# Talking-heads attention and gMLP: scores in query chunks of 64, 128, 128, 128 instead of 120, 120, 120, 88, the 64 as four 64x64 tiles

## The chip, the cores and the metric

The kernel runs on one core of one Trainium2 chip. The metric is the device time of a whole run in microseconds (us). The engines are TensorE (PE; its weight loads are shown as PEld), VectorE (DVE), ScalarE (ACT), GpSimd (POOL) and SyncE (SP), which issues nearly all DMAs. They run side by side and wait for each other by semaphores.

## What is computed

For 4 batches, 12 heads, 448 positions and head size 64 the reference is, cut to what matters:

```python
scores = scale * np.matmul(q, k.transpose(0, 1, 3, 2))        # (4, 12, 448, 448)
scores = np.einsum('bhij,hg->bgij', scores, w_pre)            # mix the heads before softmax
attn = softmax(scores)                                        # over j
attn = np.einsum('bhij,hg->bgij', attn, w_post)               # mix the heads after it
x = np.matmul(attn, v)                                        # -> (4, 448, 768)
# then a gMLP on x: w_in (768 x 1024), tanh-gelu, norm, w_sg (448 x 448), gate, w_out, + x
```

## The kernel before

**Stages of a batch.** (1) *Scores* (`qk`, `qk_mm`): for a chunk of queries and two heads, q times k by three fp16 matmuls per head (high*high, high*low, low*high). The two heads lie in the two 64-row halves of TensorE, so one **slot** of two heads is 6 matmuls of 448 columns. ACT (or DVE) rounds each head's PSUM bank to fp16 (`qk_hi`), DVE writes the rest (`qk_lo`), and SP writes both to DRAM (`write`, tile `s_d`). (2) *Premix* (`load_pair`, `premix`): ten queries are a **group** and two groups a **pair**; a pair is read back from DRAM with heads and queries on the partitions (tile `g`, a ring of 3) and multiplied by the head-mixing matrix, 12 matmuls in 64x64 tiles. (3) Softmax of a group (`slot`: maximum on DVE `nm`, exp on ACT `p`, sum and reciprocal on DVE `rs`). (4) *Postmix* (`postmix`): the first 45 groups (batch 0) in float32 with the weights scaled on POOL (`wp`), 4 matmuls a group; the later ones in fp16. ACT moves the result to `at`. (5) Attention times v (`av`, tile `ps_av`), once per block of 120 queries. (6) The gMLP of a batch, mixed into the next batch's softmax.

**Chunks.** Queries are cut in chunks of CQ = 120 (120, 120, 120, 88) for everything: q loads, scores, DRAM rows, group numbering, `av`. The blocks are taken in the order 0 to 3, but the groups of blocks 1 and 3 run backwards. A batch has 4 x 6 = 24 slots. The DRAM tiles rotate by chunk (three). The last chunk is written with 96 rows.

**The first chunk of batch 0** is special: its scores are kept in float32 (`qk_full`, one cast per head, split over ACT and DVE by the string `QKE`), and its premix is a float32 matmul (4 matmuls a pair, shown twice in the trace, x8). Its first 60 rows (`CUT` groups) are written head by head, pairs 0 to 2 are loaded, and only then the other 60 rows are written. The first `N1` = 6 heads of chunk 1 are done at the start too.

**What sets the order.** After the start, `Plan.run` is a list scheduler in Python: each step has an engine, a cost, a rank and conditions, and the plan's clocks decide the order in which instructions are emitted on each engine. The plan decides nothing at run time; each engine runs its list in order. Where the plan sees TensorE idle by more than `SPIN_GAP`, it emits **spin matmuls** (`keep_busy`, tile `ps_spin`, 128x256, on nothing) that keep the clock up. They wait for nothing and cost PE time also where the real gap is smaller. A pair's load waits in the plan until all score writes of its chunk are in (`all_pairs`); scores are ranked to be ready 8 groups before their chunk's first group (`fin`).

Of the kernel before, what the change touches and what calls it, by code (L numbers as in the profile page):

```python
# [69 lines left out]
CUT = 6  # L70
QKE = "svsvsvsvssvs"
N_Q32 = 1
# [10 lines left out]
def talking_heads_gmlp(ctx, tc, q, k, v, w_pre, w_post, w_in, g_ln, w_sg, b_sg, w_out, out):  # L83
# [20 lines left out]
    RC = [min(CQ, S - c * CQ) for c in range(NCH)]  # L104
    HG = 4
# [73 lines left out]
    s1_d = [dram.tile([CQ * H, 2 * S], F16, name=f"s1_d{i}") for i in range(3)]  # L179


    def mode_of(gen):

        name = gen.__name__
        if name == "slot":
            return "128x128" if gen.gi_frame.f_locals.get("full") else "64x128"
        return {"all_qk": "64x128", "all_premix": "64x64", "all_av": "128x64"}.get(name, "128x128")
# [433 lines left out]
    fin = [-5] + [e - K_QK - 3 for e in cstart[1:]]  # L621
# [32 lines left out]
    def qk_full(i, h, ps, eng=None):  # L654
        ev = min(CQ, q_rows(i))
        qk_place(i, h)
        e = ebox[i, h // 2 * 2].rearrange("p u t j -> p (u t j)").bitcast(F32).rearrange("p (u j) -> p u j", u=2)
        cast(e[:ev, h % 2, :], ps[:ev, :S], 1.0 / math.sqrt(D), eng)

    def qk_place(i, h):  # L660
        if h % 2 == 0:
            if (i, h) in early:
                ebox[i, h] = early[i, h].rearrange("p (u t j) -> p u t j", t=2, u=2)
            else:
                s1_out[0] += 1
# [13 lines left out]

    def write(i, h, r0, r1):  # L680
        dst = s1_d[i % 3].bitcast(F32).rearrange("(q n) j -> q n j", n=H)
        src = ebox[i, h - 1].rearrange("p u t j -> p (u t j)").bitcast(F32).rearrange("p (u j) -> p u j", u=2)
        nc.sync.dma_start(out=dst[r0:r1, h - 1:h + 1, :], in_=src[r0:r1])
        if r1 == min(CQ, q_rows(i)) and (i, h - 1) not in early:
            s1_out[0] -= 1

    def qk(i, h, rank):
        def room(h):
            if (i, h) in early:
                return 0  # L690
            if h % 2:
                return 0 if (i, h - 1) in ebox else None
            return 0 if s1_out[0] < 3 else None

        t = yield "pe", 570, rank, 0, lambda: after([seen(("q", i), ("k", chunks[i][0], h // HG)), free("wk0", "wk1")])
        banks = [work_bank("ps_qk") for _ in range(2)]
        qk_mm(i, h, [x for x, _ in banks])
        tm["qk", i, h] = tm["qk", i, h + 1] = t

        def wr(t):  # L700
            write(i, h + 1, 0, min(CQ, q_rows(i)))
            writes.setdefault(i, []).append(t)

        def evac(h, ps, name, last):
            def hi(_):
                qk_hi(i, h, ps)

            def lo(t):
                qk_lo(i, h, ps)
                give(t, name)  # L710
                tm["ev", i, h] = t

            def whole(t):
                qk_full(i, h, ps)
                give(t, name)
                tm["ev", i, h] = t

            chain(rank + K_EVAC, t, ([(None, evacs(S), whole, lambda: room(h))] if i < N_Q32
                                     else [(None, evacs(S), hi, lambda: room(h)), ("dve", 535, lo)]) + last)

        for a in range(2):
            evac(h + a, *banks[a], [("sp", 1500, wr, lambda: seen(("ev", i, h), ("ev", i, h + 1)))] * a)

    def all_qk():
        for i in range(1, len(chunks)):
            h0 = N1 if i == 1 else 0
            for h in range(h0, H, 2):
                yield from qk(i, h, fin[i - 1] + (h + 2 - h0) * (fin[i] - fin[i - 1]) / (H - h0))
# [24 lines left out]
    def premix(p):  # L753
# [8 lines left out]
        if i < N_Q32:  # L762
            terms = (wpre32, g_full(p)),
        else:
            terms = (wpre_hi, g[:, :, 0]), (wpre_hi, g[:, :, 1]), (wpre_lo, g[:, :, 0])
# [8 lines left out]
    def all_premix():  # L774
        for p, (i, _, n) in enumerate(pairs_):
            t = yield "pe", 1500 if i < N_Q32 else 570, n - 3.5, 0, lambda: after([seen(("pair", p)), past("exp", n - 1), past("exp", n - 2)])
# [484 lines left out]
    with tc.manual_schedule():  # L1261
# [175 lines left out]
```

## Time and profile before

| | |
|---|---|
| time, median of 3 runs | 632.83 us (632.11 to 633.39) |
| profiled execution, its own time | 632.48 us |
| span of that execution (first to last instruction) | 630.8 us |
| PE busy | 588.9 us (93%) |
| ACT, DVE, POOL busy | 454.6, 447.8, 369.0 us |

How to read it: "busy" is the time in which at least one instruction of the engine is in work; for PE it holds the spin matmuls as well, and a matmul's own duration overlaps the next one's, so the cost of a block of matmuls is read from its start to the start of the next block. Idle time in brackets at the end of a line is the wait just before that instruction and who ended it. Tile names have their numbers left out; `ps_s` is the premix result, `s_d` the scores in DRAM. Pairs and groups are counted from 0 at the start of the program.

### The profile page before, as it was taken

To read this page: it belongs to the slowest core of one execution; us is meant where nothing else is said; L and a number is where in the kernel's file an instruction comes from. 1 tells how busy PE (TensorE), PEld (TensorE's weight loads), DVE (VectorE), ACT (ScalarE), POOL (GpSimd) and SP (SyncE) were. 2 spreads that over 40 slices of the span, in tenths; PEclk is the share of its full clock that TensorE was granted. 3 is DMA by queue.
4 is the path that set the end of the run, shared out by engine and by line. 5 is a ranking of instruction groups with operands and counts; after the bars stand their busy time and mean duration, and the time that the engine had idled before them with its cause. 6 is when DMAs were issued, how large, how long until landed. Compare 5 with 4: busy or idle time off the path is not lost.

```text
span 630.8 us, 23210 instructions
## 1 busy us (share of the span) xinstructions
PE 588.9 (93%) x9437; PEld 395.7 (63%) x9437; DVE 447.8 (71%) x1088; ACT 454.6 (72%) x1047; POOL 369.0 (58%) x529
## 2 busy tenths in 40 slices
PE   8888988877998999999999999999999999999997
PEld 4454766656665565666675655667566756677754
DVE  3747778695699979866778889665878787545570
ACT  4645667674858989888788779787989777876332
POOL 4022443366357979966677868664787687865000
PEclk9989999989999999999999999999999999999999
DMA  9799959778388887748598656666697456440002
GB/s 198 204 263 292 280 169 238 170 211 216 117 243 240 205 216 205 219 113 265 143 257 209 167 141 180 160 175 186 183 267 208 114 160 174 121 116 3 2 1 88
DMA packets 79413, 112.23 MB, mean 178 GB/s; under 512 B 29290, under 2 KB 65802, under 8 KB 79306
## 3 DMA queue, kind: packets, MB, share of 16 engines
q1 hardware_dynamic: 79046, 110.74, 65.0%
q8 instruction: 74, 1.21, 0.8%
q14 instruction: 33, 0.27, 0.1%
q10 hardware_dynamic: 260, 0.01, 0.0%
HBM read 66.00 MB, written 44.73 MB: 176 GB/s over the span
## 4 chain that ended last, share of the span: by engine, by line
PE 64%; DVE 15%; ACT 9%; issue 5%; POOL 4%; DMA 2%; POOLq 0%; ACTq 0%; DVEq 0%
PE ps_av L959 10%; PE ps_x L991 10%; PE ps_s L770 7%; PE ps_u L991 7%; PE ps_v L991 7%; PE ps_qk L651 6%; PE at L848 6%; PE at L838 5%; DVE s L677 3%; DVE nm L783 3%; ACT p L790 2%; ACT at L316 2%; PE ps_x L1209 1%; PE at L991 1%; ACT s L316 1%
## 5 line engine op out<-in xcount | busy, mean ns | idle before, releaser
L321 POOL TENSOR_TENSOR pl<-p,ph 128x448 f16<-128x448 f32 x128 | 134.9, 1057 | 9.5 <-ACT ph L316 5.0
L316 ACT ACTIVATE at<-at 112x480 f32<-112x480 f32 x179 | 109.9, 615 | 42.3 <-PE at L838 22.8
L790 ACT ACTIVATE p<-ps_s,nm 128x448 f32<-128x448 f32 x180 | 114.1, 636 | 24.4 <-DVE nm L783 24.1
L783 DVE TENSOR_REDUCE nm<-ps_s 128x1 f32<-128x448 f32 x180 | 105.1, 616 | 27.8 <-PE ps_s L770 26.7
L677 DVE SCALAR_TENSOR_TENSOR s<-ps_qk,s 120x448 f16<-120x448 f32 (+1 forms) x172 | 100.6, 616 | 17.9 <-ACT s L316 16.1
L318 POOL TENSOR_SCALAR p<-p,rs 128x448 f32<-128x448 f32 x81 | 53.4, 659 | 61.1 <-DVE rs L796 33.2
L316 ACT ACTIVATE s<-ps_qk 120x448 f16<-120x448 f32 (+2 forms) x161 | 80.5, 543 | 11.1 <-PE ps_qk L651 10.2
L651 PE MATMUL ps_qk<-kT,qT 64*128 64x448 f16 (+1 forms) x576 | 76.4, 358 | 4.9 <-DVE wsT_hi L677 1.5
L959 PE MATMUL ps_av<-at,v 112*64 112x120 f32 (+1 forms) x1536 | 77.8, 260 | 3.2 <-DVE s L677 2.2
L959 PEld LDWEIGHTS ps_av<-at,v 112*64 112x64 f32 x1536 | 73.8, 137 | 6.8 <-DVE s L677 2.9
L848 PEld LDWEIGHTS <-ph 64*128 64x128 f16 x2160 | 52.7, 93 | 39.5 <-issue 24.6
L318 POOL TENSOR_SCALAR wp<-wpost,rs 128x60 f32<-128x60 f32 (+1 forms) x60 | 25.2, 430 | 79.7 <-DVE rs L796 61.7
L991 PE MATMUL ps_u<-xTh,wbuf 128*128 128x128 f16 (+1 forms) x768 | 64.9, 213 | 1.0 <-issue 0.5
L848 PE MATMUL at<-wpc_hi,ph 64*128 64x60 f16 x1080 | 61.0, 189 | 4.8 <-ACT at L316 4.6
L318 POOL TENSOR_SCALAR ph<-p 128x448 f16<-128x448 f32 x93 | 53.3, 573 | 18.9 <-ACT xTh L316 6.1
L991 PEld LDWEIGHTS <-wbuf 128*128 128x128 f16 x1152 | 58.8, 98 | 7.1 <-issue 5.6
L838 PE MATMUL at<-wp,p 128*112 128x120 f32 x360 | 48.2, 281 | 15.6 <-ACT at L316 8.3
L848 PE MATMUL at<-wpc_hi,pl 64*128 64x60 f16 x1080 | 59.5, 187 | 1.8 <-POOL pl L321 1.0
L848 PE MATMUL at<-wpc_lo,ph 64*128 64x60 f16 x1080 | 59.9, 187 | 0.0
L991 PE MATMUL ps_u<-xTl,wbuf 128*128 128x128 f16 (+1 forms) x384 | 59.9, 212 | 0.0
L838 PEld LDWEIGHTS at<-wp,p 128*112 128x112 f32 x360 | 41.4, 183 | 26.9 <-issue 14.6
L991 PE MATMUL ps_x<-wo,gbuf 128*128 128x384 f16 (+1 forms) x336 | 57.2, 328 | 0.0
(207 smaller groups left out, 1181.7 us busy)
## 6 DMA issues: line engine op xcount, KB each, us to landing
g<-s_d SPq DMA_DIRECT2D x176, 210.0 KB, 4.5
s_d<-s SPq DMA_DIRECT2D x62, 420.0 KB, 4.0
s_d<-s SPq DMA_DIRECT2D x24, 336.0 KB, 3.5
v<-in_v_dram SPq DMA_DIRECT2D x12, 448.0 KB, 7.9
out_dram<-ot SPq DMA_DIRECT2D x24, 192.0 KB, 4.0
q<-in_q_dram SPq DMA_DIRECT2D x11, 384.0 KB, 4.9
st<-in_k_dram SPq DMA_DIRECT2D x9, 448.0 KB, 5.0
st<-in_moe_w_out_dram SPq DMA_DIRECT2D x8, 384.0 KB, 3.4
```

The lines of the kernel that those rows point to most:

```text
L316: e.activation(out=o, in_=i, func=AF.Copy, scale=scale)
L318: e.tensor_scalar(out=o, in0=i, scalar1=scale, scalar2=1.0, op0=ALU.mult, op1=ALU.mult)
L321: (e or pl.on).tensor_tensor(out=o, in0=a, in1=b, op=ALU.subtract)
L651: nc.tensor.matmul(ps[:rows, :S], lhsT=qT2[i % 2][r, tq, h // 2, :rows], rhs=kT[r, h // HG, tk, h // 2 % 2, :], start=(n == 0), stop=(n == 2))
L677: nc.vector.scalar_tensor_tensor(out=e[:ev, h % 2, 1, :], in0=ps[:ev, :S], scalar=1.0 / math.sqrt(D), in1=e[:ev, h % 2, 0, :], op0=ALU.mul ...
L770: nc.tensor.matmul(st[m]["s2"][o:o + 64, :S], lhsT=w[rows], rhs=x[rows, u, :], start=(k == 0), stop=(k == len(terms) - 1))
L783: nc.vector.tensor_reduce(out=nm, in_=st[n]["s2"][:, :S], axis=AX.X, op=ALU.max, negate=True)
L790: nc.scalar.activation(out=x["p32"], in_=x["s2"][:, :S], func=AF.Exp, bias=x["nm"], accum_out=x["ss"])
L838: nc.tensor.matmul(ps[:TC, jc * w:(jc + 1) * w], lhsT=x["p32"][:, jc * TC:(jc + 1) * TC], rhs=x["wp"], start=True, stop=True)
L848: nc.tensor.matmul(at2[:, hf ^ glist[n][2] % 2, jc * w:(jc + 1) * w], lhsT=l[rows, js], rhs=r[rows], start=(k == 0), stop=(k == 2))
L959: nc.tensor.matmul(ps[a * D:(a + 1) * D, k3 * rows:(k3 + 1) * rows], lhsT=x[:, h, jc, :], rhs=y[:, jc, h, w:w + rows], start=(jc == 0 and ...
L991: nc.tensor.matmul(o, lhsT=l, rhs=r, start=first, stop=last)
```

## The change

- Scores of a batch are now cut at 64, 128, 128, 128 queries, in the order in which the groups are taken (`RUNS` lists, for each chunk, first row, first query, count): chunk 0 is queries 0 to 63, chunk 1 is 64 to 119 and 168 to 239, chunk 2 is 120 to 167 and 240 to 319, chunk 3 is 320 to 447. Blocks of 120 stay for groups, DRAM reads and `av`.
- The 64-query chunk does four heads at once: 12 matmuls in four 64x64 tiles, the two pairs of heads in the two halves of the PSUM partitions (a **quad**). So a batch has 3 quads and 18 slots instead of 24 slots, and 42 instead of 48 evacuations by `qk_hi` and `qk_lo`, all of 128 rows.
- A write to DRAM is one DMA for each run of queries and each pair of heads: per batch 6 + 12 + 12 + 6 = 36 instead of 24. A q load is one DMA per run. The DRAM tile is one per batch (two in turn).
- The first chunk of batch 0 is split in fp16 high and low like the others (no `qk_full`, `QKE`, `CUT`, `N_Q32`), and its premix is the fp16 one.
- A pair now waits for every chunk that has one of its queries (`need`); chunk ranks follow the first pair that needs them (`first`, `fin`). In batch 0 pairs 0 to 2 (queries 0 to 59) need chunk 0, and pair 3 (60 to 79) needs chunk 1 as well.

```diff
+    RUNS = [[(0, 0, 64)], [(0, 64, 56), (56, 168, 72)], [(0, 120, 48), (48, 240, 80)], [(0, 320, 128)]]
+    QR = [sum(n for _, _, n in x) for x in RUNS]
...
-    s1_d = [dram.tile([CQ * H, 2 * S], F16, name=f"s1_d{i}") for i in range(3)]
+    s1_d = [dram.tile([S * H, 2 * S], F16, name=f"s1_d{i}") for i in range(2)]
...
     def fetch_q(i, t):
-        b, c = chunks[i]
-        rows = min(P, S - c * CQ)
-        nc.sync.dma_start(out=t[:rows], in_=q[b, :, c * CQ:c * CQ + rows, :].rearrange("h p d -> p h d"))
+        for r, q0, n in RUNS[i % NCH]:
+            nc.sync.dma_start(out=t[r:r + n], in_=q[i // NCH, :, q0:q0 + n, :].rearrange("h p d -> p h d"))
...
-    fin = [-5] + [e - K_QK - 3 for e in cstart[1:]]
+    first = [NG] * len(chunks)
+    need = []
+    for i, t, n in pairs_:
+        q0 = chunks[i][1] * CQ + t * NT
+        q1 = min(S, q0 + min(2, GROUPS[chunks[i][1]] - t) * NT)
+        need.append([chunks[i][0] * NCH + c for c in range(NCH) if any(a < q1 and q0 < a + m for _, a, m in RUNS[c])])
+        for j in need[-1]:
+            first[j] = min(first[j], n)
+    fin = [-5] + [n - K_QK - 3 for n in first[1:]]
+    for i in range(NCH, len(chunks), NCH):
+        fin[i] = fin[i - 1] + (fin[i + 1] - fin[i - 1]) / 3
...
         for n, (tq, tk) in enumerate(((0, 0), (0, 1), (1, 0))):
-            for a, ps in enumerate(pss):
-                r = slice(a * D, (a + 1) * D)
-                nc.tensor.matmul(ps[:rows, :S], lhsT=qT2[i % 2][r, tq, h // 2, :rows], rhs=kT[r, h // HG, tk, h // 2 % 2, :],
-                                 start=(n == 0), stop=(n == 2))
+            for o in range(heads(i) // 2):
+                for a, ps in enumerate(pss):
+                    r = slice(a * D, (a + 1) * D)
+                    nc.tensor.matmul(ps[o * rows:(o + 1) * rows, :S], lhsT=qT2[i % 2][r, tq, h // 2 + o, :rows],
+                                     rhs=kT[r, h // HG, tk, h // 2 % 2 + o, :], start=(n == 0), stop=(n == 2))
...
+    def write(i, h):
+        dst = s1_d[i // NCH % 2].bitcast(F32).rearrange("(q n) j -> q n j", n=H)
+        src = ebox[i, h].rearrange("p u t j -> p (u t j)").bitcast(F32).rearrange("p (u j) -> p u j", u=2)
+        for o in range(heads(i) // 2):
+            for r, q0, n in RUNS[i % NCH]:
+                r += o * q_rows(i)
+                nc.sync.dma_start(out=dst[q0:q0 + n, h + 2 * o:h + 2 * o + 2, :], in_=src[r:r + n])
...
-                [past("pre", pairs_[p - RING + 1][2] - 1)] + (writes.get(i, []) if len(writes.get(i, ())) == H // 2 else [None])))
+                [past("pre", pairs_[p - RING + 1][2] - 1)]
+                + [x for j in need[p] for x in (writes.get(j, []) if len(writes.get(j, ())) == H // heads(j) else [None])]))
...
-        if i < N_Q32:
-            terms = (wpre32, g_full(p)),
-        else:
-            terms = (wpre_hi, g[:, :, 0]), (wpre_hi, g[:, :, 1]), (wpre_lo, g[:, :, 0])
+        terms = (wpre_hi, g[:, :, 0]), (wpre_hi, g[:, :, 1]), (wpre_lo, g[:, :, 0])
```

**SP, between the load of pair 2 and the load of pair 3** (`s_d` is the scores in DRAM, `wbuf`, `xTh`, `xTl`, `wo`, `wsT_hi`, `wsT_lo` are weight buffers that hold scores at the start, `g` the ring of pairs). The last seven rows up to the load of pair 3 before:

```order
16 L683 DMA s_d_138<-s_312 60x896
17 L683 DMA s_d_139<-wo 120x896 x2
18 L683 DMA s_d_139<-wsT_hi 120x896
19 L683 DMA s_d_139<-wsT_lo 120x896
20 L331 DMA q_94<-in_q_dram 128x12x64
21 L398 DMA v_129<-in_v_dram 112x4x256
22 L748 DMA g_122<-s_d_138 60x2x448 x2
```

and the last nine now:

```order
21 L689 DMA s_d_138<-wsT_hi 56x896
22 L689 DMA s_d_138<-wsT_hi 72x896
23 L689 DMA s_d_138<-wsT_lo 56x896
24 L689 DMA s_d_138<-wsT_lo 72x896
25 L397 DMA v_129<-in_v_dram 112x4x256
26 L1387 DMA gln<-in_moe_g_ln_dram 128x4x1
27 L1388 DMA bsg<-in_moe_b_sg_dram 128x448
28 L397 DMA v_129<-in_v_dram 112x4x256
29 L752 DMA g_122<-s_d_138 60x2x448 x2
```

Before, pair 3 read `s_d_138`, whose last row stands at 16, and the rows of chunk 1 (`s_d_139`) stood between for later pairs. Now pair 3 reads the tile that rows 21 to 24, the last heads of chunk 1, write; one more v load and two small loads stand ahead of it.

**DVE, from the softmax sums of pair 2 to the maxima (`nm`) of pair 3** (`s<-ps_qk` is the low part of a slot's scores, L1395 to L1402 set up constants). Before:

```order
50 L321 TENSOR_TENSOR qT_127<-ps_q,qT_127 128x384 x2
51 L677 SCALAR_TENSOR_TENSOR s_631<-ps_qk,s_631 120x448 x2
52 L1395 TENSOR_SCALAR gln<-gln 128x4
53 L1396 TENSOR_SCALAR bsg<-bsg 128x448
54 L1397 TENSOR_SCALAR ident_x<-ident 128x128
55 L1400 TENSOR_SCALAR mean_97<-ident_96 128x64 x2
56 L1401 SCALAR_TENSOR_TENSOR diff_98<-ident_96,mean_97 128x128
57 L1402 SCALAR_TENSOR_TENSOR mean_97<-ident_96,mean_97 128x128
58 L783 TENSOR_REDUCE nm<-ps_s_642 128x1
```

Now:

```order
46 L323 TENSOR_TENSOR qT_127<-ps_q,qT_127 128x384 x2
47 L680 SCALAR_TENSOR_TENSOR s_654<-ps_qk,s_654 128x448 x2
48 L680 SCALAR_TENSOR_TENSOR s_688<-ps_qk,s_688 128x448 x2
49 L1390 TENSOR_SCALAR gln<-gln 128x4
50 L1391 TENSOR_SCALAR bsg<-bsg 128x448
51 L1392 TENSOR_SCALAR ident_x<-ident 128x128
52 L1395 TENSOR_SCALAR mean_97<-ident_96 128x64 x2
53 L1396 SCALAR_TENSOR_TENSOR diff_98<-ident_96,mean_97 128x128
54 L1397 SCALAR_TENSOR_TENSOR mean_97<-ident_96,mean_97 128x128
55 L680 SCALAR_TENSOR_TENSOR s_728<-ps_qk,s_728 128x448 x2
56 L784 TENSOR_REDUCE nm<-ps_s_763 128x1
```

Three slots of chunk 2 (`s_654`, `s_688`, `s_728`) now stand ahead of pair 3 where one stood. On PE the same place holds 67 spin matmuls between the premix of pair 2 and that of pair 3, in four blocks, where 23 stood; in the whole program there are 202 where there were 114, all of them in the first part of batch 0.

## Rows read from the trace of the kernel before

**Rows 1.** The page: busy time, share of the span, instructions; then the chain.

```profile
PE 588.9 (93%) x9437; PEld 395.7 (63%) x9437; DVE 447.8 (71%) x1088; ACT 454.6 (72%) x1047; POOL 369.0 (58%) x529
...
PE 64%; DVE 15%; ACT 9%; issue 5%; POOL 4%; DMA 2%; POOLq 0%; ACTq 0%; DVEq 0%
```

**Rows 2.** Stretches: us, busy PE, PEld, DVE, ACT, POOL; clock, DMA share, GB/s.

```profile
25.00:45.00 20.00, 16.49 (x125) 11.26 (x125) 11.50 (x31) 10.08 (x24) 5.05 (x11) 0.92 0.97 259
...
55.00:80.00 25.00, 21.41 (x248) 15.30 (x248) 17.60 (x46) 15.16 (x36) 10.72 (x18) 1.00 0.99 292
80.00:120.00 40.00, 34.99 (x399) 26.96 (x397) 30.14 (x80) 28.48 (x69) 16.37 (x30) 1.00 0.81 207
120.00:160.00 40.00, 31.77 (x350) 23.54 (x351) 29.12 (x71) 26.36 (x64) 22.61 (x36) 0.96 0.71 183
...
280.00:320.00 40.00, 39.70 (x774) 26.21 (x775) 29.63 (x77) 33.14 (x80) 26.72 (x38) 1.00 0.73 215
...
520.00:560.00 40.00, 39.32 (x744) 25.83 (x742) 23.96 (x66) 32.53 (x77) 31.42 (x41) 1.00 0.56 161
```

**Rows 3.** PE in order of time, batch 1: start, us, what, count, [idle before].

```profile
202.84 0.75 PE L651 MATMUL ps_qk<-kT,qT 64*128 64x448 f16 x6
203.51 0.57 PE L770 MATMUL ps_s<-g,wpre_hi 60*64 60x448 f16 x8
203.92 0.36 PE L770 MATMUL ps_s<-g,wpre_lo 60*64 60x448 f16 x4
204.21 0.39 PE L991 MATMUL ps_v<-wv_hi,xTh 128*128 128x512 f16 x1
```

**Rows 4.** PE in order of time, premix of pairs 0, 2, 3, 4 and between.

```profile
27.64 0.98 PE L770 MATMUL ps_s<-g,vn_hi 60*64 60x448 f32 x8
...
35.63 0.98 PE L770 MATMUL ps_s<-g,vn_hi 60*64 60x448 f32 x8
36.55 1.89 PE L838 MATMUL at<-wp,p 128*112 128x120 f32 x16
...
48.22 0.98 PE L770 MATMUL ps_s<-g,vn_hi 60*64 60x448 f32 x8
...
50.00 2.03 PE L301 MATMUL ps_spin<-ident,ident 128*128 128x256 f16 x17
52.03 2.02 PE L770 MATMUL ps_s<-g,vn_hi 60*64 60x448 f32 x8
...
59.59 1.04 PE L838 MATMUL at<-wp,p 128*112 128x120 f32 x8 [1.65 <-ACT at L316]
```

**Rows 5.** The chain in order of time around q transposes and the first `av`.

```profile
44.41 1.02 PE ps_q L337 x6
...
74.08 5.07 PE ps_av L959 x96
79.15 0.69 PE ps_s L770 x12
```

**Rows 6.** The page's groups: evacuations of the scores (high on ACT, low on DVE).

```profile
L677 DVE SCALAR_TENSOR_TENSOR s<-ps_qk,s 120x448 f16<-120x448 f32 (+1 forms) x172 | 100.6, 616 | 17.9 <-ACT s L316 16.1
...
L316 ACT ACTIVATE s<-ps_qk 120x448 f16<-120x448 f32 (+2 forms) x161 | 80.5, 543 | 11.1 <-PE ps_qk L651 10.2
```

**Rows 7.** SP's DMA issues in order of time: start, us, tile, count.

```profile
19.13 0.31 SPq L683 DMA_DIRECT2D s_d<-s  x1
21.70 3.20 SPq L748 DMA_DIRECT2D g<-s_d  x6
...
39.18 1.11 SPq L748 DMA_DIRECT2D g<-s_d  x2
```

**Rows 8.** The page's DMA issues: KB each, median us to landing.

```profile
g<-s_d SPq DMA_DIRECT2D x176, 210.0 KB, 4.5
s_d<-s SPq DMA_DIRECT2D x62, 420.0 KB, 4.0
v<-in_v_dram SPq DMA_DIRECT2D x12, 448.0 KB, 7.9
```

More of the change, by code (lines that the diff above doesn't have):

```diff
@@ L69 @@
 TP = (24300, 26100, 27900)
-CUT = 6
-QKE = "svsvsvsvssvs"
-N_Q32 = 1
 N_W = 0
@@ new lines, in qk_place, with qk_hi, qk_lo @@
+    def qk_place(i, h):
+        if (i, h) in early:
+            ebox[i, h] = early[i, h].rearrange("p (u t j) -> p u t j", t=2, u=2)
+        else:
+            s1_out[0] += 1
+            ebox[i, h] = s1p.tile([P, 2, 2, S], F16, tag="s1", name="s1")
+    def qk_hi(i, h, a, ps, eng=None):
+        cast(ebox[i, h][:, a, 0, :], ps[:, :S], 1.0 / math.sqrt(D), eng)
+    def qk_lo(i, h, a, ps):
+        e = ebox[i, h][:, a]
+        nc.vector.scalar_tensor_tensor(out=e[:, 1, :], in0=ps[:, :S], scalar=1.0 / math.sqrt(D),
+                                       in1=e[:, 0, :], op0=ALU.mult, op1=ALU.subtract)
@@ L685, in write @@
+    def write(i, h):
[5 more added lines that the diff above has]
+                nc.sync.dma_start(out=dst[q0:q0 + n, h + 2 * o:h + 2 * o + 2, :], in_=src[r:r + n])
+        if (i, h) not in early:
             s1_out[0] -= 1
     def qk(i, h, rank):
[L688 to L693, printed above, removed]
@@ L695, in qk, with room @@
-        t = yield "pe", 570, rank, 0, lambda: after([seen(("q", i), ("k", chunks[i][0], h // HG)), free("wk0", "wk1")])
+        def room():
+            return 0 if (i, h) in early or s1_out[0] < 3 else None
+        t = yield "pe", 570, rank, 0, lambda: after([seen(("q", i), ("k", chunks[i][0], h // HG)), free("wk0", "wk1"), room()])
+        qk_place(i, h)
         banks = [work_bank("ps_qk") for _ in range(2)]
         qk_mm(i, h, [x for x, _ in banks])
-        tm["qk", i, h] = tm["qk", i, h + 1] = t
+        for a in range(heads(i)):
+            tm["qk", i, h + a] = t
@@ L700, in wr, with evac @@
         def wr(t):
-            write(i, h + 1, 0, min(CQ, q_rows(i)))
+            write(i, h)
             writes.setdefault(i, []).append(t)
-        def evac(h, ps, name, last):
+        def evac(a, ps, name, last):
             def hi(_):
-                qk_hi(i, h, ps)
+                qk_hi(i, h, a, ps)
             def lo(t):
-                qk_lo(i, h, ps)
+                qk_lo(i, h, a, ps)
                 give(t, name)
[L711 to L719, printed above, removed]
+                tm["ev", i, h + a] = t
+            chain(rank + K_EVAC, t, [(None, evacs(S), hi), ("dve", 535, lo)] + last)
@@ L726, in all_qk @@
             h0 = N1 if i == 1 else 0
-            for h in range(h0, H, 2):
-                yield from qk(i, h, fin[i - 1] + (h + 2 - h0) * (fin[i] - fin[i - 1]) / (H - h0))
+            for h in range(h0, H, heads(i)):
+                yield from qk(i, h, fin[i - 1] + (h + heads(i) - h0) * (fin[i] - fin[i - 1]) / (H - h0))
     def all_pairs(p0):
@@ L775, in all_premix @@
         for p, (i, _, n) in enumerate(pairs_):
-            t = yield "pe", 1500 if i < N_Q32 else 570, n - 3.5, 0, lambda: after([seen(("pair", p)), past("exp", n - 1), past("exp", n - 2)])
+            t = yield "pe", 570, n - 3.5, 0, lambda: after([seen(("pair", p)), past("exp", n - 1), past("exp", n - 2)])
             for m in premix(p):
@@ L1327, in qk_now @@
         def qk_now(i, h):
-            pool, tag = ((ps_wk, "wk"), (ps_ml, "ml"))[h // 2 % 2]
+            pool, tag = ((ps_wk, "wk"), (ps_ml, "ml"))[turns[1] % 2]
+            turns[1] += 1
             pss = [pool.tile([P, 512], F32, tag=tag, name="ps_qk") for _ in range(2)]
+            qk_place(i, h)
             qk_mm(i, h, pss)
             for a, ps in enumerate(pss):
-                if i < N_Q32:
-                    qk_full(i, h + a, ps, eng[QKE[h + a]])
-                else:
-                    qk_hi(i, h + a, ps, nc.scalar)
-                    qk_lo(i, h + a, ps)
+                qk_hi(i, h, a, ps, nc.scalar)
+                qk_lo(i, h, a, ps)
+            for a in range(heads(i)):
                 tm["qk", i, h + a] = 0
-            if i == 0:
-                write(i, h + 1, 0, CUT * NT)
+            write(i, h)
             writes.setdefault(i, []).append(0)
@@ L1382, in talking_heads_gmlp @@
             qk_now(1, h)
-        for h in range(0, N1, 2):
-            write(1, h + 1, 0, CQ)
         for hg in range(H // HG):
```

75 lines of the change are left out of this document (29 added, 46 removed).

## The prediction

> **What bounds the kernel now.** I read the page first: PE is busy 588.9 of 630.8 us and holds 64% of the chain that ended last [rows 1], so PE is idle for 41.9 us in all. Then the stretches show that this is two programs. From 280 on PE is full (39.7 and 39.3 of 40 us) while DVE, ACT and POOL have a fifth or more to spare [rows 2]: there each us of PE work taken away should move the end by about as much. Before 160 it is another matter: PE is idle 3.5, 3.6, 5.0 and 8.2 us in the four stretches shown, 20.3 us together, and from 25 to 80 the DMA engines are 97 to 99% busy at 259 to 292 GB/s [rows 2]. There the softmax chain, the order of the lists and the spin matmuls set the pace. So the change has to be costed twice, once as PE work and once in the first 80 us.
>
> **PE work removed.** A slot runs from 202.84 to the next block at 203.51, 0.67 us. A premix, which is 12 matmuls of 448 columns in 64x64 tiles, the very shape of a quad, runs from 203.51 to 204.21, 0.70 us [rows 3]. So four heads of 64 queries cost what two heads of 120 cost. Before: 4 x 24 = 96 slots, 64.3 us. Now 72 slots and 12 quads, 48.2 + 8.4 = 56.6 us: **-7.7 us**, 1.9 a batch. The six float32 premixes of batch 0 run 0.92 us (35.63 to 36.55) [rows 4] and become 0.70: **-1.3 us**. Together -9.0 us, if nothing else moved. The q transposes shrink for 64 rows, by less than 0.1 us a batch; I leave that out.
>
> **PE work added.** The lists hold 202 spin matmuls instead of 114. Seventeen of them took from 50.00 to 52.03, 0.12 us each [rows 4], so 88 more are **+10.6 us**, all in the first part of batch 0. A spin costs nothing where PE would have waited anyway, and its full time where it wouldn't. On this the sign of the change hangs, so I walk through the start.
>
> *To pair 0.* Before, the last score write of chunk 0 goes out at 19.13, pair 0 is loaded at 21.70 [rows 7] and premixed at 27.64 [rows 4]. Now three quads replace six slots (3 x 0.70 against 6 x 0.67, up to 1.9 us sooner), but a bank's cast is followed by DVE's low part, 0.62 each for two banks [rows 6], up to 1.2 us later. Between -1.9 and +1.2 I take 0: pair 0 again at 27.6.
>
> *Pair 0 to pair 3.* Pair 0 to 2 took 8.0 us; 19 more spins (2.3) and two cheaper premixes (-0.4) make it 9.9. Pair 2 to 3 took 12.6 us (35.63 to 48.22) [rows 4]; 44 more spins (5.3) and two more slots of chunk 2 (1.3), less 0.2, make it 19.0. Pair 3 is premixed at about 56.5, **8.3 us later than before**, of which only 1.3 is useful work. The reason is in the lists: pair 3 must now wait for all of chunk 1, the plan has it in late and fills the gap with spins.
>
> *Is the data there by then?* Before, 17.5 us passed from the load of pair 0 to that of pair 3 [rows 7]. Now the writes ahead are six of 128 rows instead of six of 60 and four of 120, and a second v load of 448 KB [rows 8] and 224 KB of constants come on top: some 420 KB more, 1.5 us at 290 GB/s [rows 2]. So the load leaves near 41 and lands 4.5 us later [rows 8], at 45 to 46, some 10 us before PE asks for it. The wait for chunk 1 is covered by spins that are longer than it; SP's queue behind it (v, the next pairs) is as full as before.
>
> A rule speaks against the new writes. What the trace shows is only that 120-row writes of 420 KB land in 4.0 us [rows 8] and that the engines are full in this stretch. The Trainium skill, "DMA: Bandwidth & Descriptors", section "Why a DMA increments its semaphore by 16 and not by 1", says a DMA runs on the largest number of engines up to 16 that divides its slow dimensions. By an estimate from that page runs of 56 and 72 rows would use 14 and 12 engines where 120 rows use 15, and chunk 1's writes would take 17% longer, 1.6 us. No run here shows that yet; with 10 us of cover the sum by it is the same.
>
> *Pair 3 to the end of the first av.* Before, 48.22 to 79.15 [rows 4, 5], 30.9 us. Now one pair fewer stands there (-0.7), three premixes are cheaper (-0.7), two groups' postmixes fewer (-2.1, at 1.04 as the row at 59.59), two slots fewer (-1.3), a set of q transposes more (+1.0, the row at 44.41 [rows 5]) and seven spins more (+0.8): 27.9 us if all its waits stay. Of these, 3.6 us are PE's idle time from 55 to 80 [rows 2], and the premix of pair 4 took 2.02 instead of 0.98 [rows 4]; without them it is 23.2. So the first av ends between 79.7 and 84.4, against 79.15. I take 80.1, **+1.0 us**, close to the lower end: 48 spins now stand between premixes and their postmixes, where the waits (1.65 at 59.59) were.
>
> **What is left after the first av.** Before: 84 pairs, 166 groups, 78 slots and a set of q transposes. Now: 85 pairs (+0.7), 168 groups (+2.1), 60 slots and 9 quads (-12.1 + 6.3), the transposes done (-1.0): **-4.0 us**. Spins left: 41 instead of 23, +2.2; as PE idles 13.2 us from 80 to 160 [rows 2], I take half as covered, **+1.1 us** (bounds 0 and 2.2).
>
> **Evacuations.** In batch 0 there are as many as before (12 single casts become 6 high and 6 low). In batches 1 to 3 there are 18 fewer of each, 18 x 0.543 = 9.8 us of ACT and 18 x 0.616 = 11.1 us of DVE [rows 6]. They lie beside a full PE and are worth only the waits that they caused: **-1.5 us** of the 21.6 us of idle time that lie outside the four early stretches, start and end of the program among it (bounds 0 and -3). SP issues 48 more writes, at 0.31 us [rows 7] 15 us over the whole program. Pair loads are queued behind them on SP, but SP mostly stands waiting for work after the start; I cost this at nothing, and at 1 us if a pair load once ends up last.
>
> **Sum.** +1.0 - 4.0 + 1.1 - 1.5 = -3.4 us. Against the profiled execution's 632.48 that is 629.1; the median of the runs lies 0.35 higher, so **629.4 us**. As a check: -9.0 of work and +10.6 of spins leave -3.4 only if 5.0 of the 41.9 us of waits go, which the 20.3 us of early waits can give.
>
> **Rivals.**
> *Spins and waits both stay (slower).* The plan's gaps are not the real ones: the spins run in full and the waits for ACT's and POOL's results come after them as before. The first av ends at 84.4, +5.3 - 4.0 + 2.2 = +3.5: **636.3**. It decides from an end of the first av later than about 83.5. For it: pair 3 comes 8 us later almost for certain, and before, the premix of pair 3 followed its spins without a wait. Against it: the waits shown are latencies between premix and postmix, which spins in between shorten.
> *The start gives it all back.* The spins only replace waits, the first av ends 1 us sooner, relief is at its bound: -1.0 - 4.0 - 3.0 = -8.0, **624.8**. For it: the lists before and now differ little from the second av on.
> *Half the late gain is off the path.* The slots saved in batches 1 to 3 (5.7 us) leave PE waiting at other points, since ACT runs at 83% [rows 2] and each group needs its chain: -3.4 + 2.9, **632.3**, no change. Against it: PE at 98 to 99% there.
> *Quads don't do what they say.* If only two of the four tiles ran at a time, a quad would cost 1.37 us: +8.0, **637.4**. Against it: the premix in the same tiles at 0.70, though its weights have 60 rows and its banks are shared otherwise.
>
> **How the numbers follow.** Chances: my case 0.42, start gives back 0.20, half the late gain lost 0.14, spins and waits both stay 0.21, quads 0.03. A difference of 0.2% (1.3 us) is about what a measurement can tell from no change. My case lies under 631.5 but for 0.02 of it, so faster is 0.40 + 0.20 = 0.60, the same 0.02 + 0.14 = 0.16, slower 0.24. The range leaves about one in ten out on each side: **622 to 636.5**, the low end a little beyond the give-back case, the high end at that of the slow one.
>
> **What would show it.** Quads: blocks of 12 score matmuls at 0.70 us from start to next start. Spins: 202, with pair 3's premix near 56 and no wait before it. The first av's end at 80 (83.5 or later: the slow rival). The load of pair 3 landing before 47. PE idle from 25 to 160 well under 20 us. From 280 on PE still at 98% or more, with batch after batch 1.9 us shorter. The prediction is wrong if pair 3's data is what PE waits for, if a stretch after 160 gains idle time, or if the pairs at a batch's first chunk wait for score writes.

## The result: 622.3 us, and the profile after

The changed kernel takes 622.27 us (621.22 to 624.90) against 632.47 for the kernel before in the same job: a ratio of 0.9843, interval [0.9809, 0.9877], about 10 us faster. The forecast was 629.4, faster, range 622.0 to 636.5. So the sign was right. That the time lies inside the range, by 0.3 us at the low end, is luck: the forecast gain of 3.4 us was a third of the real one. That is the thing to explain.

The profiled execution took 624.9 us (span 623.2); its granted clock was 0.73 in the first 25 us. A second profile of the same kernel, called `after_again` below, had a span of 623.3 and its start at the full clock; places in the first 80 us are read from that one. Both executions were the slowest of their runs, some 2.5 us above the median. The page of the changed kernel, busy time and chain, to be put beside [rows 1]:

```profile
PE 589.9 (95%) x9549; PEld 400.3 (64%) x9549; DVE 431.5 (69%) x1066; ACT 440.5 (71%) x1017; POOL 379.6 (61%) x545
...
PE 74%; DVE 11%; ACT 6%; DMA 4%; issue 3%; POOL 1%; SPq 0%; POOLq 0%; ACTq 0%; DVEq 0%
```

PE is as busy as before (+1.0 us: less work, more spins), but its idle time fell from 41.9 to 33.3 us. DVE and ACT lost 16.3 and 14.1 us of work. Stretches of the changed kernel (columns as in [rows 2]):

```profile
25.00:45.00 20.00, 15.75 (x141) 10.71 (x137) 11.50 (x30) 10.73 (x26) 5.55 (x11) 0.91 0.89 255
45.00:55.00 10.00, 10.00 (x74) 7.56 (x74) 3.51 (x8) 3.51 (x7) 0.00 (x0) 0.83 0.61 138
55.00:80.00 25.00, 23.35 (x259) 17.22 (x259) 17.50 (x49) 14.32 (x34) 5.87 (x13) 1.00 0.95 263
80.00:120.00 40.00, 35.58 (x379) 26.01 (x375) 31.95 (x85) 28.74 (x71) 19.50 (x32) 1.00 0.85 242
120.00:160.00 40.00, 34.06 (x451) 26.11 (x449) 31.74 (x77) 25.80 (x61) 21.73 (x35) 0.96 0.84 224
160.00:280.00 120.00, 112.68 (x1948) 75.01 (x1945) 99.39 (x237) 97.49 (x227) 92.01 (x122) 1.00 0.74 195
280.00:600.00 320.00, 317.55 (x6043) 215.30 (x6040) 219.12 (x552) 243.45 (x561) 227.31 (x303) 1.00 0.56 158
```

The last two stretches of the kernel before, for comparison:

```profile
160.00:280.00 120.00, 112.84 (x1949) 73.39 (x1951) 102.30 (x244) 99.96 (x233) 86.56 (x110) 1.00 0.72 198
280.00:600.00 320.00, 313.21 (x5955) 212.99 (x5956) 226.83 (x558) 249.05 (x576) 218.96 (x291) 1.00 0.60 161
```

From 25 to 160 PE idles 16.3 us where it idled 20.3 in the four stretches of [rows 2]. From 280 to 600 it idles 2.45 us where it idled 6.79. I had called that part of the program full and allowed 1.5 us for all idle time outside the early stretches.

PE in order of time around pairs 0 and 3 and the first `av` (`after_again`; then the block behind the first `av` in the first profile):

```profile
27.36 0.35 PE L771 MATMUL ps_s<-g,wpre_hi 60*64 60x448 f16 x1 [1.22 <-DMA g<-s_d]
28.33 0.57 PE L771 MATMUL ps_s<-g,wpre_hi 60*64 60x448 f16 x7 [0.62 <-DMA g<-s_d]
...
38.58 0.57 PE L771 MATMUL ps_s<-g,wpre_hi 60*64 60x448 f16 x8
...
47.95 0.74 PE L665 MATMUL ps_qk<-kT,qT 64*128 64x448 f16 x6
48.63 2.03 PE L303 MATMUL ps_spin<-ident,ident 128*128 128x256 f16 x17
...
53.90 2.03 PE L303 MATMUL ps_spin<-ident,ident 128*128 128x256 f16 x17
55.86 0.57 PE L771 MATMUL ps_s<-g,wpre_hi 60*64 60x448 f16 x8
...
74.66 5.14 PE L960 MATMUL ps_av<-at,v 112*64 112x120 f32 x96
79.73 0.57 PE L771 MATMUL ps_s<-g,wpre_hi 60*64 60x448 f16 x8
```

```profile
81.67 0.57 PE L771 MATMUL ps_s<-g,wpre_hi 60*64 60x448 f16 x8
```

Pair 0 waits twice for its load (1.22 and 0.62 us), which I had not foreseen. Pair 3 is premixed at 55.86 (forecast 56.5) with no wait of its own, and the first `av` ends at 79.73 (forecast 80.1). So the start as a whole came out as worked, 8 us of delay for pair 3 included. What I missed lies behind the first `av`: 543.6 us are left from there to the end, against 551.7 before. That is -8.1; the terms behind it in my sum were -4.0 + 1.1 - 1.5 = -4.4. In the first profile 541.5 us are left behind 81.67, which is -10.2. Most of the difference is a stretch of `after_again` from 440 to 460, with a granted clock of 0.91 where the first profile has 1.00: eight matmuls of `ps_v` start 0.43 us apart there instead of 0.22. So the late gain is 8 to 10 us.

### The profile page after: what moved, and what is told of

Its sections match the earlier page's. It is cut to its first block, busy times and chain, and to the rows that moved or that the text cites. A ratio compares the mean times of both kernels' runs of the same rounds, so it can differ in the third digit from the quotient of the medians.

```text
span 623.2 us, 23425 instructions
## 1 busy us (share of the span) xinstructions
PE 589.9 (95%) x9549; PEld 400.3 (64%) x9549; DVE 431.5 (69%) x1066; ACT 440.5 (71%) x1017; POOL 379.6 (61%) x545
## 4 chain that ended last, share of the span: by engine, by line
PE 74%; DVE 11%; ACT 6%; DMA 4%; issue 3%; POOL 1%; SPq 0%; POOLq 0%; ACTq 0%; DVEq 0%
PE ps_x L992 13%; PE ps_av L960 12%; PE ps_s L771 8%; PE at L849 7%; PE ps_u L992 7%; PE ps_v L992 7%; PE ps_qk L665 6%; PE at L839 5%; DVE s L680 3%; PE ps_spin L303 2%; DVE nm L784 2%; ACT at L318 2%; PE ps_x L1210 2%; PE at L992 1%; DMA xTl<-in_moe_w_in_dram 1%
## 5 line engine op out<-in xcount | busy, mean ns | idle before, releaser
L323 POOL TENSOR_TENSOR pl<-p,ph 128x448 f16<-128x448 f32 x128 | 132.8, 1039 | 11.2 <-ACT ph L318 5.2
L680 DVE SCALAR_TENSOR_TENSOR s<-ps_qk,s 128x448 f16<-128x448 f32 x150 | 87.3, 616 | 11.4 <-ACT s L318 9.5
L320 POOL TENSOR_SCALAR wp<-wpost,rs 128x60 f32<-128x60 f32 (+1 forms) x64 | 27.5, 441 | 85.0 <-DVE rs L797 69.7
L318 ACT ACTIVATE s<-ps_qk 128x448 f16<-128x448 f32 x141 | 70.1, 546 | 8.9 <-PE ps_qk L665 8.8
L320 POOL TENSOR_SCALAR p<-p,rs 128x448 f32<-128x448 f32 x82 | 52.7, 644 | 38.6 <-DVE rs L797 17.5
L665 PE MATMUL ps_qk<-kT,qT 64*128 64x448 f16 (+1 forms) x576 | 69.8, 370 | 4.1 <-DVE s L680 2.5
L320 POOL TENSOR_SCALAR ph<-p 128x448 f16<-128x448 f32 x99 | 57.2, 577 | 24.8 <-PE at L849 10.4
L796 DVE TENSOR_SCALAR rs<-ss 128x1 f32<-128x1 f32 x180 | 26.8, 149 | 44.4 <-ACT p L791 43.3
L992 PE MATMUL ps_x<-wo,gbuf 128*128 128x384 f16 (+1 forms) x336 | 55.9, 328 | 0.0
```

The costliest lines, as they stand in the source:

```text
L318: e.activation(out=o, in_=i, func=AF.Copy, scale=scale)
L320: e.tensor_scalar(out=o, in0=i, scalar1=scale, scalar2=1.0, op0=ALU.mult, op1=ALU.mult)
L323: (e or pl.on).tensor_tensor(out=o, in0=a, in1=b, op=ALU.subtract)
L665: nc.tensor.matmul(ps[o * rows:(o + 1) * rows, :S], lhsT=qT2[i % 2][r, tq, h // 2 + o, :rows], rhs=kT[r, h // HG, tk, h // 2 % 2 + o, :], ...
L680: nc.vector.scalar_tensor_tensor(out=e[:, 1, :], in0=ps[:, :S], scalar=1.0 / math.sqrt(D), in1=e[:, 0, :], op0=ALU.mult, op1=ALU.subtract)
L992: nc.tensor.matmul(o, lhsT=l, rhs=r, start=first, stop=last)
```

## The experiments

Twelve runs in three jobs. The kernel before took 631.98, 632.2 and 633.03 us in them, so kernels of different jobs are compared by their ratios to it; 1% is 6.3 us.

| run | time | ratio to before, interval |
|---|---|---|
| after_again: the changed kernel | 622.8 | 0.9846 [0.9821, 0.9871] |
| quad_serial: other order in a quad | 623.2 | 0.9863 [0.9839, 0.9887] |
| quad_twice: quads issued twice | 627.1 | 0.9919 [0.9893, 0.9944] |
| two_heads: quads undone | 631.9 | 1.0002 [0.9983, 1.0020] |
| evac_halves: quads evacuated in halves | 642.5 | 1.0159 [1.0137, 1.0182] |
| halves_planned: the same, known to the plan | 642.4 | 1.0168 [1.0146, 1.0190] |
| few_spins: 18 spins for 202 | 625.5 | 0.9897 [0.9876, 0.9918] |
| dma33: one number of the plan | 612.0 | 0.9691 [0.9668, 0.9713] |
| dma30: the same, further | 614.8 | 0.9711 [0.9682, 0.9741] |
| two_heads_dma33: both | 628.0 | 0.9939 [0.9914, 0.9964] |
| before_dma33: the number in before | 636.5 | 1.0054 [1.0024, 1.0083] |
| before_split: the split alone | 636.5 | 1.0059 [1.0036, 1.0082] |

The theory to test: the gain is the quads' PE work and fewer evacuations, and I had charged the spins too much. The rival: the gain is in the new chunks and in the lists that came with them.

### after_again: the changed kernel once more

> The changed kernel once more, as the measure for the other three on the same chip. Both theories: 621 to 623 us, some 10 us under the kernel before.

0.9846: the result stands.

### quad_serial: the tiles of a quad in another order

```diff
-        for n, (tq, tk) in enumerate(((0, 0), (0, 1), (1, 0))):
-            for o in range(heads(i) // 2):
+        for o in range(heads(i) // 2):
+            for n, (tq, tk) in enumerate(((0, 0), (0, 1), (1, 0))):
```

> The same 12 matmuls of each quad with the two loops exchanged: first all six of the upper two heads, then all six of the lower two. All instruction lists stay as they are but for the order inside the 12 quads. Theory (the gain after the start is PE time of quads): if only two tiles are then at work at a time, a quad takes about 1.3 us instead of 0.70, and of the 12 x 0.6 = 7.5 us nearly all shows, 5 to 8 us slower than the changed kernel. Rival (the gain is in the relief of ACT and DVE by fewer evacuations, PE's share lies beside it): under 3 us slower.

One quad and the premix behind it, first in the changed kernel, then in this run:

```profile
134.01 0.76 PE L665 MATMUL ps_qk<-kT,qT 64*64 64x448 f16 x12
134.61 0.55 PE L771 MATMUL ps_s<-g,wpre_hi 60*64 60x448 f16 x8
```

```profile
133.79 0.78 PE L665 MATMUL ps_qk<-kT,qT 64*64 64x448 f16 x12
134.38 0.56 PE L771 MATMUL ps_s<-g,wpre_hi 60*64 60x448 f16 x8
```

From start to start a quad takes 0.60 us in the changed kernel and 0.59 here, so the edit did not take the four tiles apart and says nothing on the price of a quad run two tiles at a time. What it shows: between these two orders there is no difference, and a quad costs 0.60, a little less than the 0.70 that I had taken from a premix [rows 3]. The Trainium skill, "TensorEngine Tiling (Array Packing)", section "Key Properties", says that tiles work independently of each other; these rows agree.

### quad_twice: what PE work costs there

```diff
-        for n, (tq, tk) in enumerate(((0, 0), (0, 1), (1, 0))):
+        for n, (tq, tk) in [*enumerate(((0, 0), (0, 1), (1, 0)))] * (heads(i) // 2):
```

> The changed kernel with the 12 matmuls of each of the 12 quads issued twice in a row (the second time over the first, so the result is the same); every other instruction and the order on each engine is that of the changed kernel (622.8 us when last run). It prices the quads' own PE time on the path. If a quad costs what its blocks show (0.60 us) and PE is what sets the end, +12 x 0.60 = +7.2: 630. If the quads lie where PE waits anyway, for evacuations or for data, less than half of it is seen: 623 to 626. If two of four tiles run at a time after all, the doubled quads take 1.3 us more each: +15, 638.

```profile
134.08 1.39 PE L665 MATMUL ps_qk<-kT,qT 64*64 64x448 f16 x24
135.24 0.61 PE L771 MATMUL ps_s<-g,wpre_hi 60*64 60x448 f16 x8
```

The doubled quad takes 1.16 us, 0.56 more; twelve of them 6.7 us. The time rose by 0.73%, 4.6 us (2.3 to 6.9 with both intervals). So most of the PE time of the quads, perhaps all, is on the path, and the case of two tiles at a time is out.

### two_heads: the quads undone, all else kept

```diff
-        return 4 if QR[i % NCH] == 64 else 2
+        return 2
```

with evacuations of 64 rows for this chunk and one call more for each quad at the start.

> The changed kernel with one part undone: the chunk of 64 queries goes two heads at a time, 24 slots of 6 matmuls with 64 rows in place of 12 quads; chunks, DRAM layout and waits stay, and the plan knows it. PE then has 24 x 0.67 - 12 x 0.60 = +8.9 us more, ACT 24 x 0.54 = +13 and DVE 24 x 0.62 = +15 us more, in the batches' first chunks. If PE work alone sets the time: 622.8 + 8.9 = 631.7. If the evacuations of the first chunk hold PE up as well (the 20 us that halved evacuations cost with lists not made for them): 638 or more. If the lists absorb half of the PE work: 627. If the gain of the change lies in the new chunks and not in the quads: 623.

631.9: the whole gain is gone, and the rest of the change taken together is worth nothing (1.0002). The quads are worth 1.56%, 9.9 us (7.9 to 11.8). This includes the 24 evacuations of each kind that the quads save, so in my sum they stood for -7.7 - 1.5 = -9.2. The other edits, which my sum charged with +5.8, cost nothing together. How the 9.9 us divide between PE time and evacuations is not shown: PE's busy time is 593.2 us here, 3 to 5 more than in the two profiles of the changed kernel and not 8.9; the rows at the end, where slots of 64 rows overlap with the premix behind them, fit that. The end of the first `av`, and the stretch from 280 to 600:

```profile
79.05 0.57 PE L773 MATMUL ps_s<-g,wpre_hi 60*64 60x448 f16 x8
```

```profile
280.00:600.00 320.00, 319.07 (x6032) 214.32 (x6023) 226.40 (x563) 250.50 (x577) 226.61 (x301) 1.00 0.58 160
```

The first `av` ends where it did before the change (79.15), with all 202 spins on PE. From 280 to 600 PE idles 0.9 us where it idled 6.8 before the change, though this kernel has as many slots and evacuations in a batch as the kernel before, and DVE and ACT are as busy (226.4 and 250.5 us against 226.8 and 249.1). So it is not the relief of ACT and DVE that took the late idle time away.

### evac_halves and halves_planned: the evacuations

```diff
-        cast(ebox[i, h][:, a, 0, :], ps[:, :S], 1.0 / math.sqrt(D), eng)
+        n = q_rows(i)
+        for r in range(0, P, n):
+            cast(ebox[i, h][r:r + n, a, 0, :], ps[r:r + n, :S], 1.0 / math.sqrt(D), eng)
```

and the same for the low part; `halves_planned` doubles the plan's two costs for it as well.

> The evacuations of the 64-query chunks as two instructions of 64 rows instead of one of 128, high and low, so that a batch has 48 of each again as before the change; the lists are otherwise the same, quads run in four tiles. It puts 24 x 0.54 = 13 us back on ACT and 24 x 0.62 = 15 us on DVE. Theory (PE time is the gain, relief is worth 1.5 to 4 us): 1 to 5 us slower than the changed kernel. Rival (relief is the gain): 7 to 10 us slower, about as the kernel before.

> The changed kernel with each evacuation of a quad as two instructions of 64 rows, as in the run before that took 642.5 us, but now the plan knows that they take twice as long. PE's work is that of the changed kernel; ACT has 13 and DVE 15 us more. If the 20 us of that run were a matter of lists not made for it, 622.8 to 626. If evacuations beside a full PE cost as such, 632 or more. My prediction's term for 18 evacuations of each kind fewer was 1.5 us (0 to 3), so 24 more of each would be +2 (0 to +4): 623 to 627.

Both take 20 us more than the changed kernel, so lists made without knowing it were not the reason, and the expectation of 2 us was wrong. But `two_heads` has as many evacuations of 64 rows and is 10 us faster than these, although it has more matmul work. So the number of evacuations alone does not cost so much; where they stand is the likelier reason. Part of it lies in the start: pair 0 is premixed at 35.3 and 34.9 instead of 27.4, and the first `av` ends 5.8 and 5.4 us later than in `after_again`. The rest lies behind. Here two high and two low parts share a bank, one behind the other. DVE's forms in `halves_planned` (x, busy, mean ns), and PE at the second quad of batch 1:

```profile
L684 DVE SCALAR_TENSOR_TENSOR s<-ps_qk,s 128x448 f16<-128x448 f32 x132 | 76.9, 617 | 8.6 <-ACT s L318 7.2
L684 DVE SCALAR_TENSOR_TENSOR s<-ps_qk,s 64x448 f16<-64x448 f32 x36 | 22.4, 621 | 1.6 <-ACT s L318 0.8
```

```profile
141.17 0.76 PE L665 MATMUL ps_qk<-kT,qT 64*64 64x448 f16 x11 [0.83 <-DVE s L684]
142.65 0.38 PE L775 MATMUL ps_s<-g,wpre_hi 60*64 60x448 f16 x2 [0.71 <-ACT p L795]
145.48 0.56 PE L775 MATMUL ps_s<-g,wpre_hi 60*64 60x448 f16 x6 [2.46 <-ACT p L795]
```

Half the rows take as long (621 against 617 ns). The quad waits 0.83 us for a low part, and the premix behind it 0.71 and 2.46 us for ACT's exp, which stands behind the extra casts in ACT's list. From 120 to 160 PE does 30.84 us of work where the changed kernel did 34.06. That the holding of the bank and the casts in front of the exp make the late part is argued from such rows; no run took one of them alone.

### few_spins: are the spins on the path?

```diff
-            spin(ps_ml.tile([P, 512], F32, tag="ml", name="ps_spin"), n)
+            spin(ps_ml.tile([P, 512], F32, tag="ml", name="ps_spin"), 1)
```

> Each of the 18 blocks of planned spin matmuls cut to a single one: 18 instead of 202, all lists otherwise the same. It takes 184 x 0.12 = 22 us of spins out of the first 130 us. Theory (spins are longer than the waits that they fill, pair 3 stands some 9 us behind its data): 4 to 9 us faster than the changed kernel, if the granted clock holds. Rival (the spins only fill waits, or keep the clock up): within 2 us, or slower with a granted clock that falls in the first 130 us.

184 spins fewer, 22 us of PE at 0.12 each, and the kernel is 3.2 us slower (0.51%, 1.1 to 5.3 us). The stretch from 25 to 80, then three rows of PE, in this run:

```profile
25.00:80.00 55.00, 40.15 (x295) 23.34 (x296) 30.91 (x80) 27.09 (x64) 10.75 (x22) 0.78 0.85 243
```

```profile
49.28 1.19 PE L665 MATMUL ps_qk<-kT,qT 64*128 64x448 f16 x6 [0.87 <-DVE qT L323]
50.40 0.28 PE L303 MATMUL ps_spin<-ident,ident 128*128 128x256 f16 x1
...
56.40 0.96 PE L771 MATMUL ps_s<-g,wpre_hi 60*64 60x448 f16 x8
```

and the same stretch of the changed kernel:

```profile
25.00:80.00 55.00, 49.22 (x505) 36.38 (x507) 32.55 (x86) 27.25 (x66) 13.30 (x27) 0.97 0.88 250
```

Pair 3 comes at 56.40 without the spins and at 55.86 with them, and the first `av` ends at 82.92 instead of 79.73. Where they stood, PE now waits for `qT` and the evacuations: from 25 to 80 it idles 14.9 us instead of 5.8. And without them the granted clock of the stretch is 0.78 instead of 0.97, between the levels of 1.2 and 2.4 GHz, and a slot takes 1.12 us (49.28 to 50.40) where it took 0.68. So the 202 spins together have no net price here; they pay. The run changes waits and clock at once: what a spin costs while the clock stays up, it does not show.

### dma33 and dma30: pair 3 sooner

If spins are not what makes pair 3 late, the order of the list is: three slots of chunk 2 stand ahead of it (above), because the plan thinks that its data is late. One number tells the plan otherwise:

```diff
-T0 = dict(pe=22300, act=23100, dve=23900, pool=15200, sp=30000, dma=36000)
+T0 = dict(pe=22300, act=23100, dve=23900, pool=15200, sp=30000, dma=33000)
```

(`dma30`: 30000.)

> The changed kernel with the plan's clock for the DMA queue at the start set 3 us earlier (one number), so that the plan expects pair 3 sooner: 41 spins and one postmix more in place of 67 spins ahead of it, and 186 spins in all. If pair 3 at 56 us is late because of three chunk-2 slots and their evacuations that the plan put ahead of it, it comes at 52 to 53 now, the first av ends 2 to 4 us sooner and the time is 619 to 621. If its softmax chain is held up by other things (POOL's weights, the first v), the time stays at 622 to 623. If the data of pair 3 is not there, PE waits for it, 624 or more.

> The changed kernel with the plan's DMA clock 6 us earlier instead of 3: 75 spins and 15 slots ahead of pair 3 where the 612.0 us version has 87 spins and 16 slots, 155 spins in all. If there is still slack between the landing of pair 3's data (about 47) and its premix (51.6), another 1 to 2 us: 610 to 611. If the chain of postmixes and chunk-2 slots ahead of it sets pair 3 now, the same 612. If the data is late, PE waits for it with a spin block less ahead: 613 to 615.

PE in `dma33` at pair 3 and at the first `av`, and its late stretches:

```profile
50.95 0.74 PE L665 MATMUL ps_qk<-kT,qT 64*128 64x448 f16 x6
51.62 0.57 PE L771 MATMUL ps_s<-g,wpre_hi 60*64 60x448 f16 x8
...
69.75 5.14 PE L960 MATMUL ps_av<-at,v 112*64 112x120 f32 x96
74.82 0.57 PE L771 MATMUL ps_s<-g,wpre_hi 60*64 60x448 f16 x8
```

```profile
160.00:280.00 120.00, 116.84 (x2024) 74.91 (x2022) 102.16 (x245) 101.43 (x235) 92.28 (x117) 1.00 0.74 201
280.00:600.00 320.00, 318.60 (x5965) 216.09 (x5958) 217.75 (x540) 236.78 (x543) 219.42 (x292) 1.00 0.54 153
```

612.0 us, the fastest kernel of the study: 1.55% or 9.8 us below the changed kernel and 3.1% below the kernel before. Pair 3 comes 4.2 us sooner and the first `av` ends 4.9 us sooner. The expectation stopped there, at 619 to 621. (The trace holds 168 spins, not the 186 of the expectation.) Another 4 us lie between 160 and 280, where PE idles 3.2 us instead of 7.3: the new lists happen to wait less there. `dma30` gains nothing more (0.9711, the intervals overlap): pair 3 comes at 52.59 there, 1 us later than in `dma33`.

### before_dma33 and two_heads_dma33: is that a gain of the number alone?

The same line changed in the kernel before, and in `two_heads`.

> The kernel before with the same one number changed as in the run of the changed kernel that took 612.0 us (the plan's clock for the DMA queue 3 us earlier): 90 spins instead of 114, and no spins between the postmixes and pair 3. It tells whether those 10 us belong to the new chunks or to the plan's clock. In the kernel before, pair 3 is loaded at 39.2 and its premix stands at 48.2, so it can come at most some 4 us sooner. If the lists after the start repeat the gain, as they did in the changed kernel, 622; if only the start's own gain comes through, 628 to 630; if the data of pair 3 is not there so soon, 632 or more.

> The changed kernel with both: the 64-query chunk two heads at a time (24 slots in place of 12 quads, which took 631.9 against 622.8) and the DMA clock 3 us earlier (612.0). If the quads are worth their PE time whatever the start does, 612.0 + 9.1 = 621. If part of the 9.1 was luck of the lists, it comes out elsewhere: 612 to 617, or over 625.

The kernel before gets slower by it, 0.54%. PE there, and SP's issue of the load that it waits for:

```profile
36.13 1.90 PE L838 MATMUL at<-wp,p 128*112 128x120 f32 x16
42.72 1.51 PE L337 MATMUL ps_q<-ident,q 128*128 128x128 f32 x6 [4.69 <-DMA q<-in_q_dram]
```

```profile
35.19 1.21 SPq L331 DMA_DIRECT2D q<-in_q_dram  x1
```

The list puts the q transposes of chunk 2 first, and their data is not there: 4.69 us of wait with the postmixes behind it. In the changed kernel that load is issued at 32.22, ahead of the last score writes:

```profile
32.22 1.42 SPq L330 DMA_DIRECT2D q<-in_q_dram  x2
```

So of the two numbers the old one is better for the old start and the new one for the new. `two_heads_dma33`, with 0.9939, is only 3.9 us faster than the kernel before, and the quads are worth 2.48%, 15.7 us, between it and `dma33` instead of 9.9. All of it lies behind the first `av`, which ends at 74.71 here and at 74.82 in `dma33`. Its stretch from 160 to 280:

```profile
160.00:280.00 120.00, 111.27 (x1863) 69.73 (x1865) 95.05 (x227) 94.20 (x218) 87.26 (x114) 0.97 0.69 190
```

PE idles 8.7 us there, 5.5 more than in `dma33`; that is about the 6 us by which the two prices of the quads differ. The lists more likely than the quads make this part; then a list can give or take some 5 us. Why `dma33` got the good one is not settled.

### before_split: one part of the change alone

```diff
-N_Q32 = 1
+N_Q32 = 0
```

> The kernel before with one part of the change done alone: the first chunk's scores are split in fp16 high and low like the others and premixed in fp16, chunks of 120 kept. My prediction's terms for this part: six premixes 1.3 us cheaper, up to 1.2 us more for the low parts at the start. So 630.5 to 632.5. If the cast and the low part on the way to the first load are not covered, 634; if the new lists give or take as much as the plan's clock did (10 us), outside 628 to 636.

0.59%, 3.7 us, slower: 636.5 lies outside 628 to 636, where I had put the case that new lists give or take much. The first `av` ends at 76.18, 3 us sooner than before, so the loss comes after it. PE from 120 to 160, and what it waits for there:

```profile
120.00:160.00 40.00, 28.46 (x335) 21.76 (x336) 31.41 (x80) 26.82 (x65) 21.09 (x35) 1.00 0.74 184
```

```profile
PE at L838 <- POOL wp L318: 7.0, 5, 1.8
```

PE does 3.3 us less in this stretch than before (31.77 in [rows 2]), far behind the first chunk, and its wait for POOL was 3.2 us before: the start's gain is lost again in the lists, which also hold 149 spins instead of 114. If the parts add up, the new chunks and their waits win about as much back, since all of the change but the quads is worth 0; no run had them alone.

## Why the prediction was right in sign and too small

By its own steps:

- **PE work removed (-7.7 for the quads).** Right, a little small: 0.60 us a quad (`quad_serial`, `after_again`) makes it -8.9 for twelve by the blocks; undoing them cost 9.9 (7.9 to 11.8) with their evacuations, against -9.2 in the sum, and 15.7 under the lists of `dma33`.
- **The start.** Pair 0 at 27.4 to 28.3 (27.6), pair 2 at 38.6 (37.5), pair 3 at 55.9 (56.5) without a wait, its load issued at 41.8 (near 41), the first `av` at 79.7 (80.1). The end came out as worked, in part by luck: `two_heads`, without quads, has it at 79.05, so the three quads of the start won nothing, where I had up to -1.9, and the rest of the change cost nothing, where I had +2.9. The 56-row and 72-row writes did not become what PE waits for at pair 3; the 1.6 us estimated for them were not measured.
- **The rest of the change (+5.8): the step that failed.** I took +10.6 us for 88 more spins and -1.3 for the premixes, and let only 5.0 us of PE's waits go, 3.5 of them on this side: +5.8 for all that is not quads. `two_heads` measures that sum at 0.0 (-1.1 to +1.3). In the changed kernel 8.6 us of waits went, as the idle time fell from 41.9 to 33.3. To the end of the first `av` the rest cost 0 instead of +2.9; behind it 550.0 us are left in `two_heads` against 551.7 before, -1.6 where I had +1.8 for pairs and groups and +1.1 for spins. So spins that stand in front of a wait were priced too high, as `few_spins` bears out for all of them together, and idle time from 280 on that I had bounded at 3 us went as well.
- **What is left after the first av (-4.0), later spins (+1.1), evacuations (-1.5).** Together -4.4; measured -8.1 to -10.2. Of the 3.7 to 5.8 us between, about 0.9 are the nine late quads at 0.60 instead of 0.70, and 1.1 the later spins if they had no price. The idle time from 280 to 600 gives 2.8 more: it fell by 4.3 where I had allowed 1.5 for everything outside the early stretches. The groups of the evacuations in the changed kernel, beside [rows 6]:

```profile
L680 DVE SCALAR_TENSOR_TENSOR s<-ps_qk,s 128x448 f16<-128x448 f32 x150 | 87.3, 616 | 11.4 <-ACT s L318 9.5
...
L318 ACT ACTIVATE s<-ps_qk 128x448 f16<-128x448 f32 x141 | 70.1, 546 | 8.9 <-PE ps_qk L665 8.8
```

  DVE's group is 13.3 us smaller and ACT's 10.4. But that relief is not what the 4.3 us need, as `two_heads` idles even less there without it. They go with the new chunks: the three kernels with the old ones (`before`, `before_dma33`, `before_split`) idle 6.3 to 6.8 us from 280 to 600, those with the new ones 0.9 to 3.1, but for `evac_halves` (7.8), whose list does not know its evacuations. Which edit of the new chunks does it, their bounds, their waits or their ranks, stays open.
- **The rivals.** "Spins and waits both stay" fell: no wait behind the spins. "Two at a time" fell: 0.60. "Half the late gain is off the path" fell, the late part gained more than its work. "The start gives it all back" came nearest in time (624.8): its late waits went, but the first `av` did not end sooner.

## What to carry to other kernels

Do not price filler matmuls by their duration: ask whether the instruction behind them would have started sooner without them, and what clock it would then have had. After a change to a statically scheduled kernel, set the planner's clocks anew: here the number kept from the old start cost the new one 9.8 us, as much as the whole change had won (half of it by the end of the first `av`, the rest in lists whose luck is not explained), and the number that is better for the new start made the old one slower. And such a list may move the time by some 5 us for no reason that the edit tells, so a term is best measured by undoing it under two lists.

## What the runs showed of the hardware

- An evacuation's time did not go by its rows: 64 rows of 448 columns took 621 ns on DVE and 128 rows 617. So a bank filled to 128 rows by four 64x64 tiles halves the evacuations of 64-row scores.
- Matmuls in different 64x64 tiles overlapped in both orders of issue that were tried (0.60 and 0.59 us a quad), across different work too. In `two_heads` a slot of 64 rows and the premix behind it start in turns:

```profile
132.40 0.38 PE L665 MATMUL ps_qk<-kT,qT 64*64 64x448 f16 x2
132.42 0.38 PE L773 MATMUL ps_s<-g,wpre_hi 60*64 60x448 f16 x2
132.61 0.35 PE L665 MATMUL ps_qk<-kT,qT 64*64 64x448 f16 x2
132.63 0.36 PE L773 MATMUL ps_s<-g,wpre_hi 60*64 60x448 f16 x2
```
